# The first queries' load and transposes, moved from GpSimd and float16 to SyncE and float32

## The chip, the cores and the metric

The kernel runs on one core of a Trainium2 chip. A core has five engines with instruction streams of their own: TensorE (PE, matmuls; its weight loads are shown apart as PEld), VectorE (DVE), ScalarE (ACT), GpSimd (POOL) and SyncE (SP, which only issues DMAs here). Sixteen DMA engines move data between the chip's memory (HBM) and the core's SBUF. The metric is the device time of one execution in microseconds, less being better; a value given for a kernel is the median of its runs.

## The reference

Two stages follow each other. The first is an attention over blocks: a Sinkhorn normalization turns `sort_net` into soft permutations, which mix the blocks of keys and values; then each block of queries attends to one mixed block. The second is a mixture of four two-layer networks, weighted by normalized probabilities.

```python
def _attn_ref(q, k, v, sort_net):          # q, k, v: (4, 8, 768, 64); sort_net: (4, 8, 8, 8)
    P = sort_net
    for _ in range(5):
        P = np.exp(P - np.max(P, axis=-1, keepdims=True))
        P = P / (np.sum(P, axis=-1, keepdims=True) + 1e-09)
        P = P / (np.sum(P, axis=-2, keepdims=True) + 1e-09)
    k_sorted = np.einsum('bhij,bhjcd->bhicd', P, k_b)   # k_b, v_b: blocks of 96 rows
    v_sorted = np.einsum('bhij,bhjcd->bhicd', P, v_b)
    scores = scale * np.matmul(q_b, k_sb.transpose(0, 1, 2, 4, 3))
    attn = softmax(scores)                               # over the 96 keys of the block
    return np.matmul(attn, v_sb)

def _moe_ref(x, domain_probs, w1, w2):     # x: (3072, 512); w1: (4, 512, 1024); w2: (4, 1024, 512)
    p = domain_probs / (domain_probs.sum(-1, keepdims=True) + 1e-09)
    out = np.zeros((N, D))
    for e in range(4):
        out += p[:, e:e + 1] * (np.maximum(x @ w1[e], 0.0) @ w2[e])
    return out
```

All inputs and the output are float32 in HBM. `x` is the attention's output with the heads of a token side by side.

## The kernel before

The instructions of each engine run in the order in which the kernel's text issues them; semaphores are put in where one engine needs what another or a DMA has made. No scheduler moves anything. There are two sets of PSUM buffers, `psM` and `psA`, of two buffers each, handed out in turn.

**Loads.** GpSimd issues nearly all loads, since those cast float32 to float16 on the way (`load_natural` for k and v, `load_half_queries` for batch 0's queries, `load_w1` and `load_w2` for the networks' weights). Its DMAs use eight semaphores in turn, so from the ninth on an issue also waits until the DMA eight places before it has landed. SyncE issues loads without a cast, stores and DMA transposes. At the start SyncE issues `sort_net` into `sn` (L77), then the probabilities twice, in two layouts: `p_in` (L170) and `p_own` (L171). GpSimd issues, in this order: the first halves of the queries of quads 0 and 1 (L172, through L152; a quad is four heads), the first k quad (L173), then it makes the identity matrix `ident` in float16 (L177), and issues the first v quad, the second k quad, the second v quad (L178 to L180), and four pieces of the first network's `w1` (L183).

The queries of batch 0 lie in `q0`, a view of the scratch tile `Tt[3]`: partitions 0 to 63 hold quad 0, 64 to 127 quad 1, and on each of them are two halves of the sequence, four heads, six blocks' rows and 64 columns of float16.

**Start.** PE has nothing to do until the Sinkhorn iterations are through. `warm(n)` (L272) issues `n` matmuls of a constant tile, 128x128 by 128 columns, whose result nobody reads. The text issues `warm(84)` (L307), then the five iterations (L309 to L327): an exponential on ScalarE (L310), then on VectorE row sums, reciprocal, product, column sums, reciprocal (L315 to L319) and, but for the last iteration, another product (L321). After iterations 1 to 3, VectorE also takes one step each of `spread_weights` (L244): the sum over `p_in` (L246), an addition (L248) and a reciprocal (L250). In the last iteration, between the exponential and the row sums, the text issues `h_q(0, 0, nc.scalar.copy)` and `h_q(1, 0, nc.scalar.copy)` (L313) and `warm(30)`.

`h_q` (L280) transposes the half queries of a quad: 24 transposes of 64x64 on PE (L288), through `ident`, into one PSUM tile, and one copy of it by ScalarE into `qT0[qd]` (L292).

**What follows.** After the iterations VectorE and GpSimd write half of the normalized matrix each, spread over 16 columns (L330); PE transposes it (`r_half`, L342), VectorE builds block-diagonal matrices from it (`build_PI0`, L353), and PE mixes k and v with these, quad by quad (`mix_half`, L521). Scores (`h_s`, L576), exponentials (L582), the transposes of v (`h_w`, L548), the products with v (`h_a`, L593) and the transposes of the result (`h_x`, L624) follow, and from about 18 us on the first layer of network 0 (`group0`, L704) is put between them. `h_s` reads `qT0`. The second halves of the queries are loaded at L1405, into the other half of `q0`, and transposed near 29 us by `h_q_both`. The tile `room` takes outputs of network 0 later on (L747).

All else (the other batches' attention and the networks, whose products are built from fewer block products with sums of blocks) fills the rest of the span with matmuls.

Of the kernel before, what the change touches and what calls it, by code (L numbers as in the profile page):

```python
# [10 lines left out]
F32 = mybir.dt.float32  # L11
# [7 lines left out]
def kernel(  # L19
# [11 lines left out]
    nc = tc.nc  # L31

    B, H, S, D = q.shape
# [6 lines left out]
    P = 128  # L40
# [3 lines left out]
    R = BLK // CP  # L44
# [23 lines left out]
    def psa(shape, dtype, name):  # L68
        state["n"] += 1
        return psA.tile(shape, dtype, tag="ps", name=name)  # L70
# [16 lines left out]
    def from_spare(n):  # L87
        at = spare["at"]
        spare["at"] += n
        return Sflat[:, ds(at, n)]  # L90
# [5 lines left out]
    q0 = Tt[3].rearrange("p a f x -> p (a f x)").rearrange("p (f h r d) -> p f h r d", f=2, h=4, r=R)  # L96
# [4 lines left out]
    room = const.tile([P, 4, Dm], F32, name="room")  # L101
    arena = const.tile([P, 4 * NW + NQ + 4 * 4 * P + R * 4 * VW], F16, name="arena")

    def half_queries(qd, hf):
        return q[0, ds(4 * qd, 4)].rearrange("h (p r) d -> p h (r d)", r=R)[ds(64 * hf, 64)]

    def load_natural(b, nm, qd, parts=1, between=None):
        src = {"k": k, "v": v}[nm]
        t = arena[:, ds(("k", "v").index(nm) * 2 * NW + qd * NW, NW)].rearrange("p (h r d) -> p h r d", h=4, r=R)
        natural[(b, nm, qd)] = t  # L110
        n = 4 // parts
        for m in range(0, 4, n):
            nc.gpsimd.dma_start(
                t[:, ds(m, n)].rearrange("p h r d -> p h (r d)"),
                src[b, ds(4 * qd + m, n)].rearrange("h (p r) d -> p h (r d)", r=R),
            )
            if m == 0 and between:
                between()
# [31 lines left out]
    def load_half_queries(hf):  # L150
        for qd in range(2):
            nc.gpsimd.dma_start(  # L152
                q0[ds(64 * qd, 64), hf].rearrange("p h r d -> p h (r d)"), half_queries(qd, hf)
            )
# [7 lines left out]
    def p_part(at, n):  # L162
        return Tt[2].rearrange("p a f x -> p (a f x)")[:, ds(2 * at, 2 * n)].bitcast(F32)
# [3 lines left out]
    p_den = p_part(2 * E * NT, NT).rearrange("p (t o) -> p t o", o=1)  # L167
    p_own = p_part(2 * E * NT + NT, R * E).rearrange("p (t e) -> p t e", e=E)
    own_den = p_part(2 * E * NT + NT + R * E, R).rearrange("p (t o) -> p t o", o=1)
    nc.sync.dma_start(p_in, moe_domain_probs.rearrange("(p t) e -> p t e", t=NT))  # L170
    nc.sync.dma_start(p_own, moe_domain_probs[0:S].rearrange("(t p) e -> p t e", p=P))  # L171
    load_half_queries(0)  # L172
    load_natural(0, "k", 0)  # L173


    ident = const.tile([P, P], F16, name="ident")
    make_identity(nc, ident)  # L177
    load_natural(0, "v", 0)  # L178
    load_natural(0, "k", 1)
    load_natural(0, "v", 1)  # L180
# [63 lines left out]
    def spread_weights():  # L244

        nc.vector.tensor_reduce(p_den, p_in, AX.X, ALU.add)  # L246
        yield
        nc.vector.tensor_scalar(out=p_den, in0=p_den, scalar1=1e-9, scalar2=None, op0=ALU.add)  # L248
        yield
        nc.vector.reciprocal(p_den, p_den)  # L250
        yield
        nc.vector.tensor_tensor(
            p_out.rearrange("p e t -> p t e"), p_in, p_den.broadcast_to([P, NT, E]), ALU.mult
        )
        p_rows = p_dram.rearrange("e (p t) -> p e t", t=NT)
        nc.sync.dma_start(p_rows[0:S_P], p_out[0:S_P])
        pbs[(0, 0)] = load_p(0, 0)
        nc.sync.dma_start(p_rows[S_P:P], p_out[S_P:P])
        yield
# [12 lines left out]
    def warm(n):  # L272
        ps = psM.tile([P, 4, P], F32, tag="ps", name=f"ps_w_{state['n']}")
        state["n"] += 1
        for m in range(n):
            nc.tensor.matmul(ps[:, m % 4, :], dummy, dummy, start=True, stop=True)

    qT0 = [from_spare(2 * S).rearrange("p (s f r x) -> p s f r x", s=2, f=2, r=R) for _ in range(2)]

    def h_q(qd, hf, copy, ps=None):  # L280

        if ps is None:
            ps = psa([P, 2, R, 64], F16, f"ps_q_{qd}_{hf}")
        rows = ds(64 * qd, 64)
        for sg in range(2):
            for r in range(R):
                for hh in range(2):
                    nc.tensor.transpose(  # L288
                        ps[ds(D * hh, D), sg, r, :], q0[rows, hf, 2 * sg + hh, r, :], ident[rows, rows]
                    )  # L290
        if copy:
            copy(qT0[qd][:, :, hf], ps[:])  # L292

    def h_q_both(hf, copy):

        ps = psa([P, 2, 1024], F16, f"ps_q_{hf}")
        pss = [ps[:, qd, 0:2 * R * 64].rearrange("p (s r x) -> p s r x", s=2, r=R) for qd in range(2)]
        for qd in range(2):
            h_q(qd, hf, None, pss[qd])
        for qd in range(2):  # L300
            copy[qd](qT0[qd][:, :, hf], pss[qd])
# [2 lines left out]
    srow = const.tile([GH, NB, 1], F32, name="srow")  # L304
    scol = const.tile([GH, NB, 1], F32, name="scol")
    sn16 = const.tile([GH, NB, NB, CP], F16, name="sn16")
    warm(84)  # L307
    p_steps = spread_weights()
    for it in range(5):  # L309
        nc.scalar.activation(sn[:], sn[:], AF.Exp, bias=0.0, scale=1.0)  # L310
        if it == 4:
            for qd in range(2):
                h_q(qd, 0, nc.scalar.copy)  # L313
            warm(30)
        nc.vector.tensor_reduce(srow[:], sn[:], AX.X, ALU.add)  # L315
        nc.vector.reciprocal(srow[:], srow[:])
        nc.vector.tensor_tensor(sn[:], sn[:], srow[:].broadcast_to([GH, NB, NB]), ALU.mult)
        nc.vector.tensor_reduce(scol[:], sn[:].rearrange("p i j -> p j i"), AX.X, ALU.add)
        nc.vector.reciprocal(scol[:], scol[:])  # L319
        if it < 4:  # L320
            nc.vector.tensor_tensor(  # L321
                sn[:], sn[:],
                scol[:].rearrange("p j o -> p o j").broadcast_to([GH, NB, NB]),
                ALU.mult,
            )
            if it:
                next(p_steps)  # L327
# [1146 lines left out]
    def load_w2_part(e, d):  # L1474
# [6 lines left out]

    later = [
        [(h_q_both, 1, (vec, act)), (h_w, 1, vec)],
        [(h_s, 0, 2), (h_s, 1, 2)],
        [(h_w, 0, vec)],
# [92 lines left out]
```

## Time and profile before

| | |
|---|---|
| median of 3 runs | 358.08 us (358.04 to 359.21) |
| profiled execution | 358.21 us |
| its span | 356.3 us |
| PE busy | 350.4 us |
| VectorE, ScalarE, GpSimd busy | 277.5, 170.1, 137.6 us |

The profile is that of one execution. Its span runs from the first to the last instruction of the program; 1.9 us of the execution's time lie around it. A row of a timeline reads: start in us, duration in us, engine, line of the kernel, operation, written tile <- read tiles, shapes, count, and in brackets the engine's idle time before it and what ended it. The view of waits sums such idle times. "Landing" is the time from a DMA's issue to its arrival.

### The profile page before, as it was taken

Reading aid. Unit: us, or ns where it says so; the run is one execution under the profiler, and the core shown is the slowest. Engines: PE = TensorE matmul, PEld = TensorE weight load, DVE = VectorE, ACT = ScalarE, POOL = GpSimd, SP = SyncE. Lnnn points to the kernel's source line nnn. Section 1 sums busy time; section 2 is a strip of 40 time slices with the busy share of each in tenths; the row PEclk is TensorE's granted clock in tenths of the full one; section 3 lists DMA queues with packets and bytes.
Section 4 is the critical chain, followed back from the end, with each engine's and each line's share of the span. In section 5 each row is a group of like instructions: output and inputs, shape, how many; then the busy total and the mean of one; then the engine's idle time right before and its main releaser. Section 6 shows DMA issues by size and latency. Waiting matters only on the chain.

```text
span 356.3 us, 9511 instructions
## 1 busy us (share of the span) xinstructions
PE 350.4 (98%) x3948; PEld 305.5 (86%) x3948; DVE 277.5 (78%) x555; ACT 170.1 (48%) x302; POOL 137.6 (39%) x154
## 2 busy tenths in 40 slices
PE   8899999999999999999999999999999999999996
PEld 8686857888888888988899888888888888888886
DVE  5766787779798687778879988896678886588963
ACT  2653330452425445368847259830288611598301
POOL 8766112466022420000626318840068800188400
PEclk9999999999999999999999999999999999999999
DMA  8999999999999999743995410005200014100021
GB/s 104 203 205 230 212 209 194 207 195 167 195 180 166 195 116 203 138 88 44 180 205 91 107 74 0 2 1 136 78 26 3 2 37 141 62 0 2 0 75 46
DMA packets 74762, 40.26 MB, mean 113 GB/s; under 512 B 41568, under 2 KB 70496, under 8 KB 74720
## 3 DMA queue, kind: packets, MB, share of 16 engines
q0 software_dynamic: 38720, 19.93, 43.2%
q1 hardware_dynamic: 35856, 19.67, 27.2%
q8 instruction: 31, 0.51, 0.6%
q14 instruction: 11, 0.09, 0.1%
q10 hardware_dynamic: 144, 0.07, 0.1%
HBM read 41.88 MB, written 6.34 MB: 135 GB/s over the span
## 4 chain that ended last, share of the span: by engine, by line
PE 95%; DVE 3%; issue 0%; DMA 0%; ACT 0%; DVEq 0%
PE ps_h L815 18%; PE ps_Q L1296 18%; PE ps_p L799 12%; PE ps_X L1153 10%; PE ps_Z L1153 7%; PE ps_Q L1153 7%; PE ps_Z L1296 6%; PE ps_h L704 3%; PE ps_o L741 3%; PE ps_p L860 3%; PE ps_a L479 2%; PE ps_s L444 2%; PE ps_k L425 1%; PE ps_v L391 1%; PE ps_mv L521 1%; PE ps_a L593 0%
## 5 line engine op out<-in xcount | busy, mean ns | idle before, releaser
L815 PE MATMUL ps_h<-xT,w 128*128 128x256 f16 x576 | 67.5, 273 | 0.0
L815 PEld LDWEIGHTS <-w 128*128 128x128 f16 x576 | 55.2, 98 | 7.3
L821 DVE SCALAR_TENSOR_TENSOR Hb<-ps_h,pb 128x1024 f16<-128x1024 f32 x34 | 41.5, 1223 | 17.8 <-PE ps_h L815 17.6
L1153 PEld LDWEIGHTS <-w 128*128 128x128 f16 x480 | 43.6, 98 | 4.7
L1166 POOL TENSOR_TENSOR arena<-tmp,pb 128x512 f16<-128x512 f32 x12 | 15.2, 1276 | 65.7 <-PE ps_Z L1153 49.8
L1296 PEld LDWEIGHTS <-Hb 128*128 128x128 f16 x320 | 31.1, 98 | 3.5
L1165 ACT ACTIVATE tmp<-tmp 128x512 f32<-128x512 f32 x46 | 29.0, 632 | 3.9 <-DVE tmp L1203 3.9
L1296 PEld LDWEIGHTS <-Sb 128*128 128x128 f16 x304 | 28.2, 98 | 3.0
L1153 PEld LDWEIGHTS <-arena 128*128 128x128 f16 x312 | 27.7, 98 | 2.8
L451 ACT ACTIVATE ET<-ps_s 96x768 f16<-96x768 f32 x24 | 18.1, 802 | 25.2 <-PE ps_s L444 25.0
L434 ACT CAST kT<-ps_k 64x384 f16<-64x384 f32 x48 | 22.7, 473 | 13.3 <-PE ps_k L425 12.3
L126 POOL DMA_DIRECT2D arena<-in_q_dram x24 | 19.9, 842 | 20.8 <-DMA q_ring<-arena 17.7
L1153 PE MATMUL ps_X<-ET,arena 128*128 128x256 f16 x168 | 25.2, 272 | 0.0
L1296 PE MATMUL ps_Q<-w,Hb 128*128 128x256 f16 x192 | 24.6, 273 | 0.0
L799 PEld LDWEIGHTS <-Hb 128*128 128x128 f16 x232 | 21.9, 98 | 3.0
L1159 DVE SCALAR_TENSOR_TENSOR Hb<-ps_X,pb 128x512 f16<-128x512 f32 x27 | 18.7, 692 | 7.0 <-PE ps_X L1153 7.0
L1173 ACT COPY ps_X<-ps_Z 128x512 f32<-128x512 f32 x27 | 15.4, 571 | 17.8 <-PE ps_Z L1153 17.8
L1153 PE MATMUL ps_Z<-xT,w 128*128 128x256 f16 (+1 forms) x176 | 22.5, 258 | 0.0
L785 DVE TENSOR_TENSOR Sb<-Hb 128x512 f16<-128x512 f16 x33 | 20.6, 646 | 0.0
L1180 ACT COPY tmp<-ps_X 128x512 f32<-128x512 f32 x26 | 15.2, 586 | 9.2 <-PE ps_X L1153 6.6
L1159 DVE SCALAR_TENSOR_TENSOR Hb<-ps_Z,pb 128x512 f16<-128x512 f32 x27 | 18.4, 683 | 1.3 <-PE ps_Z L1153 1.3
L1203 DVE TENSOR_TENSOR tmp<-ps_Q,tmp 128x512 f32<-128x512 f32 x26 | 17.7, 683 | 0.8 <-PE ps_Q L1153 0.8
(270 smaller groups left out, 744.3 us busy)
## 6 DMA issues: line engine op xcount, KB each, us to landing
w<-in_moe_w_dram POOLq DMA_DIRECT2D x4, 1024.0 KB, 27.2
w<-in_moe_w_dram POOLq DMA_DIRECT2D x6, 512.0 KB, 19.7
arena<-in_k_dram POOLq DMA_DIRECT2D x7, 384.0 KB, 7.6
arena<-in_v_dram POOLq DMA_DIRECT2D x7, 384.0 KB, 8.1
vs<-arena SPq DMA_DIRECT2D x36, 66.0 KB, 5.3
arena<-in_q_dram POOLq DMA_DIRECT2D x24, 96.0 KB, 7.5
out_dram<-ob SPq DMA_DIRECT2D x9, 256.0 KB, 2.0
pb<-p_dram SPq DMA_DIRECT2D x4, 512.0 KB, 5.8
```

The costliest lines, as they stand in the source:

```text
L126: nc.gpsimd.dma_start(t[:, h // 2, :, h % 2, :], q[b, h].rearrange("(t p) d -> p t d", p=P))
L434: nc.scalar.copy(kT[ds(D * hh, D), r], pk[ds(D * r, D), hh].rearrange("p a (i c) -> p a i c", c=CP),)
L451: nc.scalar.activation(ETs[2 * (pr % 2) + hh][:, 0:S].rearrange("c (a x) -> c a x", a=2), pss[hh][0:BLK, :, 0:HS], AF.Exp, bias=0.0, scale ...
L785: tt(sm[0], blk(0, 1), blk(1, 1), ALU.add)
L799: nc.tensor.matmul(ps, lhs(e, f), Ts[e][rhs][:, f, :], start=(first and e == es[0] and f == 0), stop=(done and e == es[-1] and f == KH - 1 ...
L815: nc.tensor.matmul(ps[:, f, :], w1sb[e][:, kc, ds((4 * g + f) * P, P)], xT[:, kc, ds(2 * c * P, 2 * P)], start=(kc == 0), stop=(kc == NKC ...
L821: nc.vector.scalar_tensor_tensor(out=Hb[:, homes.get(e, e), ds(4 * g, 4), :], in0=ps[:], scalar=0.0, op0=ALU.max, in1=weights(e).broadcast ...
L1153: nc.tensor.matmul(dst[:, ds(f * cols, cols)], a[lhs][:, k, ds((f0 + f) * P, P)], t[rhs][:, k, :], start=(first and f == 0 and k == 0), st ...
L1159: nc.vector.scalar_tensor_tensor(out=home(i, j), in0=src.rearrange("p (f x) -> p f x", f=m), scalar=0.0, op0=ALU.max, in1=weight(j).broadc ...
L1165: nc.scalar.activation(src, src, AF.Relu, bias=0.0, scale=1.0)
L1203: tt(t12, Q, u2, ALU.add)
L1296: nc.tensor.matmul(ps, lhs(e, f), Ts[e][rhs][:, f, part], start=(first and e == 0 and f == 0), stop=(e == E - 1 and f == KH - 1), skip_gro ...
```

## The change

The first half of quad 0's queries is no longer loaded by GpSimd with a cast. SyncE loads it as float32, as its second DMA, into `q32`: partitions 0 to 63 of `q0`, both halves of the sequence's room, read as float32. GpSimd's DMA for quad 1 stays. GpSimd also copies a 64x64 corner of `ident` into a corner of `room` as float32, `ident32`. A new function `h_q32` transposes quad 0's half queries by 24 float32 matmuls (the queries as stationary operand, `ident32` as the moving one) into a float32 PSUM tile. It is issued ahead of the iterations, behind `warm(60)` in the place of `warm(84)`. In the last iteration ScalarE copies its result into `qT0[0]`, quad 1's transposes follow as before, and `warm(28)` stands for `warm(30)`. The second half of quad 0's queries is still loaded at the same place, over `q32`.

```diff
+    q32 = q0[0:64].rearrange("p f h r d -> p (f h r d)").bitcast(F32).rearrange("p (h r d) -> p h r d", h=4, r=R)
+    nc.sync.dma_start(q32.rearrange("p h r d -> p h (r d)"), half_queries(0, 0))
     nc.sync.dma_start(p_in, moe_domain_probs.rearrange("(p t) e -> p t e", t=NT))
     nc.sync.dma_start(p_own, moe_domain_probs[0:S].rearrange("(t p) e -> p t e", p=P))
-    load_half_queries(0)
+    nc.gpsimd.dma_start(q0[ds(64, 64), 0].rearrange("p h r d -> p h (r d)"), half_queries(1, 0))
     load_natural(0, "k", 0)
     ident = const.tile([P, P], F16, name="ident")
     make_identity(nc, ident)
+    ident32 = room[0:64, 0, 0:64]
+    nc.gpsimd.tensor_copy(ident32, ident[0:64, 0:64])
     load_natural(0, "v", 0)
...
+    def h_q32():
+
+        ps = psa([P, 2, 512], F32, "ps_q32")
+        for sg in range(2):
+            for r in range(R):
+                for hh in range(2):
+                    nc.tensor.matmul(
+                        ps[ds(D * hh, D), sg, ds(r * 64, 64)], q32[:, 2 * sg + hh, r, :], ident32, start=True, stop=True
+                    )
+        return ps[:, :, 0:R * 64].rearrange("p s (r x) -> p s r x", r=R)
...
-    warm(84)
+    warm(60)
+    ps_q32 = h_q32()
     p_steps = spread_weights()
     for it in range(5):
         nc.scalar.activation(sn[:], sn[:], AF.Exp, bias=0.0, scale=1.0)
         if it == 4:
-            for qd in range(2):
-                h_q(qd, 0, nc.scalar.copy)
-            warm(30)
+            nc.scalar.copy(qT0[0][:, :, 0], ps_q32)
+            h_q(1, 0, nc.scalar.copy)
+            warm(28)
```

## The prediction

> **What bounds the kernel now.** I read the page first: engines, granted clock, chain.
>
> ```profile
> span 356.3 us, 9511 instructions
> PE 350.4 (98%) x3948; PEld 305.5 (86%) x3948; DVE 277.5 (78%) x555; ACT 170.1 (48%) x302; POOL 137.6 (39%) x154
> PEclk9999999999999999999999999999999999999999
> ```
>
> TensorE (PE) is busy 98% of the span at the full granted clock. The table of windows then tells where the other 2% lies; its columns are the stretch, its length, and each engine's busy time in it.
>
> ```profile
> 0.00:10.00 10.00, 8.94 (x159) 8.80 (x160) 6.18 (x30) 2.96 (x7) 8.70 (x19) 1.00 0.87 113
> 10.00:20.00 10.00, 8.17 (x204) 6.88 (x202) 6.95 (x19) 6.08 (x11) 7.67 (x19) 1.00 1.28 204
> 20.00:40.00 20.00, 19.89 (x351) 14.87 (x348) 12.92 (x25) 9.30 (x13) 10.92 (x14) 1.00 1.23 219
> 40.00:60.00 20.00, 20.00 (x162) 14.18 (x161) 17.47 (x29) 4.84 (x6) 3.02 (x5) 1.00 1.32 203
> ```
>
> From 40 us on PE has no idle time that this view shows. What the change touches lies before 17 us, so it can move the end only by moving the point from which PE runs without a break. The chain of waits shows what sets that point (columns: start, duration, what).
>
> ```profile
> 10.64 0.20 DVE scol L319
> 10.86 0.69 DVE sn L330
> 11.55 0.05 issue
> 11.60 0.26 PE ps_R L342 x4
> ```
>
> Up to 11.55 the chain is the Sinkhorn iterations on VectorE and ScalarE. No query and no TensorE work is in it. What PE does beside them is in PE's timeline:
>
> ```profile
> 1.06 6.74 PE L276 MATMUL ps_w<-Hb 128*128 128x128 f16 x84 [1.06 <-DVE Hb L157]
> 7.73 0.85 PE L288 MATMUL ps_q<-ident,T 64*64 64x64 f16 x48
> 8.51 1.85 PE L276 MATMUL ps_w<-Hb 128*128 128x128 f16 x30
> 11.60 0.26 PE L342 MATMUL ps_R<-ident,sn 32*128 32x32 f16 x4 [1.24 <-DVE sn L330]
> 14.40 0.57 PE L521 MATMUL ps_mk<-Sb,arena 128*64 128x64 f16 x24
> 16.15 0.57 PE L521 MATMUL ps_mv<-Sb,arena 128*64 128x64 f16 x24
> ```
>
> The 48 transposes of the first queries start right behind the 84 dummies: they waited for no load. PE then idles 1.24 us for the Sinkhorn result. The last two lines are the first uses of the second k and v quads. Their loads, by the DMA view cut to the issue of each (columns: KB, us from issue to landing):
>
> ```profile
> arena<-in_k_dram POOLq DMA_DIRECT2D x1, 384.0 KB, 9.3
> arena<-in_v_dram POOLq DMA_DIRECT2D x1, 384.0 KB, 10.5
> T<-in_q_dram POOLq DMA_DIRECT2D x1, 192.0 KB, 4.3
> ```
>
> k was issued at 4.88 and landed at 14.2, v at 5.62 and 16.1, the second quad's queries at about 1.93 and 6.2. All landed before their use, but v by only 0.05 us.
>
> **The change part by part.**
>
> *Dummies and float16 transposes that go (PE).* The 30 dummies took 1.85 us with the last one's latency of about 0.2 inside, so 0.056 each. 24 of the first batch's last dummies are 1.34 us; the 60th ends at 7.73 - 1.34 = 6.39. Half of the 48 transposes is about 0.4 (0.85 / 48 = 17.7 ns each), two later dummies 0.11. Removed: 1.85 us, all in PE's shadow of the Sinkhorn chain.
>
> *Float32 transposes that come (PE).* No row shows a float32 matmul. In the compiled program each of the 24 is two weight loads and two matmuls, 48 of each. Bounds: the float16 pairs give 48 x 17.7 ns = 0.85 us. If nothing overlapped, each pair would cost its weight load and its matmul in full; the line of L288 gives these:
>
> ```profile
> L288 PEld LDWEIGHTS <-T x48: 103/110/110, 7.7 to 8.4; 64*64 64x64 f16 x48
> L288 PE MATMUL ps_q<-ident,T x48: 192/193/213, 7.7 to 8.4; 64*64 64x64 f16 x48
> ```
>
> That is 48 x 0.30 = 14.4 us, an end which no PE row comes near, since each of them overlaps loads with matmuls. I take twice to four times the float16 price, as elements are twice as wide and the two halves of one tile can't run side by side as two neighbouring tiles do: 1.7 to 3.4 us, middle 2.5.
>
> *The room for it.* From 6.39 to 11.60 are 5.21 us; less 0.4 for the remaining float16 transposes, 0.1 for a change of shape, and 28 x 0.056 = 1.56 for the later dummies, 3.15 us are left, 131 ns for each float32 transpose. At 2.5 us PE ends at about 10.95 and still waits 0.65 us for the Sinkhorn result: cost 0. At 3.4 us it is 0.25 late. The cover is the Sinkhorn chain; whatever PE exceeds 3.15 us by moves everything behind it.
>
> The row says 0.85 us when 48 float16 pairs are the measure. [...]
>
> *Queries' load on SyncE's queue.* 384 KB instead of 192, since nothing is cast. Issued at 1.21, behind the 8 KB of sort_net and ahead of both probability loads; it takes an issue of 0.40 us there, so p_in goes out at about 1.66 and p_own at 2.1. Landing: the output stores of the same queue land 256 KB in 2.0 us, so 3.0 us for 384 KB at the quick end (4.2); the gpsimd query load's 4.3 us is the slow end (5.5). The DMA share is 0.22 to 0.35 between 2 and 3.5 us, so I take the quick end. The transposes begin at 6.39: cost 0 at either.
>
> *p_in behind it.* VectorE's reduction of p_in stands in the Sinkhorn chain's engine order, at 5.72; everything of the chain is queued behind it. p_in's packets ran 2.5 to 3.0 us; behind the queries it lands at 4.7, or 6.0 at the slow end. Cost 0, bound 0.3. p_own is first used at 21.1.
>
> *GpSimd's queue.* One DMA issue less (0.66), one 64x64 copy more (about 0.3, by the 0.29 of the 128x128 copy, L194): 0.4 us earlier for all behind it. The identity in float32 is there by about 4. GpSimd's half of L330 began at 11.23, 0.4 after its input; it would end at 12.1 instead of 12.46, but PE comes to it at 13.33 behind two blocks of matmuls. Gain 0. The k and v loads come up to 1.0 us earlier (192 KB at about 192 KB per us), and with them the weight loads, whose issues wait for them. Since PE waited for none, gain 0, bound -1.0. The copy of room's corner is read long before room is next written, past 31 us.
>
> *ScalarE.* The first evacuation reads float32: by the 0.81 of the 768-wide L582 against 0.73, +0.08. It ends near 11.1; ScalarE's next work is at 13.05 after 2.08 us idle. Cost 0, unless PE is over 2 us late.
>
> *Sum.* 358.21 us for the profiled execution (span 356.3 and 1.9 around it) + 0. The median of the runs shown is 358.08, so 358.1 is forecast. 0.5%, 1.8 us, is about what a measurement of this kernel can tell from no change.
>
> **The rivals.**
>
> *PE is late (slower).* The float32 weight loads do not hide behind matmuls. Price: 48 x 0.103 = 4.94 on the 1.70 us, 6.6 in all, 3.5 us over the room: 361.6. It decides from 131 ns for each transpose, and passes 0.5% at (3.15 + 1.8) / 24 = 206 ns. For it: alternating tiles hid the float16 loads, while here the second load of a tile comes while its first half still runs. Against it: L521 hides its loads at 15 to 16 ns for each matmul at the same 64 columns.
>
> *p_in is late (slower).* SyncE's queries run into gpsimd's stream, and the chain stands at 5.72. Worked above: up to 0.3, and 0.9 if its 8 packets on each DMA engine also take turns with gpsimd's 0.08 us ones: 358.4 to 359.0.
>
> *The clock falls (slower).* If the float32 phase is short, PE is idle from 9.3 to 11.6, 2.3 us instead of 1.24. If the granted clock fell to half there, as it visibly was for the first dummies (38 in the first 3.94 us, about 0.105 each against 0.056), some 1.7 to 3.4 us of matmuls between 11.6 and 15.6 would be added: 359.8 to 361.5. The row shows no fall over 1.24 us. [...]
>
> *The loads did matter (faster).* If the 0.05 us of slack of v hides a wait, the ramp gains up to the 1.0 us of the stream: 357.1. Against it: the gap before 16.15 is the ordinary 0.09 us of a change of shape.
>
> **How the numbers follow.** PE in time, 358.1: 64%. PE late: 22%, 5 of them under 1.8 us and 17 beyond, as no row fixes the price. p_in late: 5%, 1 beyond. Clock: 4%, beyond. Loads: 5%, 2 of them beyond 0.5% by more than I can work out. So faster 2%, same 64 + 5 + 4 + 3 = 76%, slower 22%. The range goes from 357.0, the loads' gain, to 360.6, where float32 transposes take 0.235 us each (5.65 us, 2.5 over the room); left out are some 10 of PE late, 2 of the clock and 2 below.
>
> **What would show it.** In the changed kernel's PE timeline: float32 transposes starting at about 6.4 straight behind the dummies, lasting 1.7 to 3.4 us, and a line L342 (moved in number) at 11.6 still released by VectorE. VectorE's reduction of p_in at 5.7 without idle time. k and v landing up to 1.0 us earlier with no PE start moved. Wrong it would be if L342 starts late behind PE's own work, if the Sinkhorn steps shift, or if PE's dummies after 11.6 take 0.1 us each.

## The result and the profile after

The changed kernel takes 360.74 us (median of 6 runs, 360.14 to 361.38) against 358.15 us (6 runs, 358.04 to 359.21). The ratio is 1.0067, with a 95% interval of 1.0050 to 1.0085: slower, by 2.6 us. The forecast was no change, 358.1 us, in a range from 357.0 to 360.6. The median lies 0.1 us above that range; the ratio times the 358.08 us from which the forecast was counted gives 360.5, just inside it. So the kernel is slower where no change was forecast, by more than the 0.5% which the prediction called the same.

The profiled execution took 360.42 us with a span of 358.2 us, 1.9 us more than before. PE's busy time did not grow:

```profile
span 358.2 us, 9510 instructions
PE 350.5 (98%) x3946; PEld 305.7 (85%) x3946; DVE 277.5 (77%) x555; ACT 170.1 (47%) x302; POOL 137.5 (38%) x154
PEclk9899999999999999999999999999999999999999
```

Two things stand there already: the same matmul time in a longer span, so PE waits more, and one slice of the granted clock (the second, 9 to 18 us) below full speed. The chain of waits has a DMA in it now (columns: start, duration, what):

```profile
1.21 0.74 SPq L171
...
2.00 4.90 DMA T<-in_moe_domain_probs_dram
...
6.92 0.25 DVE T L250
...
11.99 0.69 DVE sn L346
...
12.73 0.26 PE ps_R L358 x4
```

SyncE's issue of the queries comes first, then p_in's DMA, then VectorE's sum over it, then the rest of the Sinkhorn iterations. Lines have moved: L250 was L246, L346 was L330, L358 was L342. The wait is in VectorE's timeline, with its idle time and its cause in brackets:

```profile
5.85 0.21 DVE L337 TENSOR_TENSOR sn<-sn,scol 32x64 f32<-32x64 f32 x1
6.92 0.25 DVE L250 TENSOR_REDUCE T<-T 128x24 f32<-128x96 f32 x1 [0.86 <-DMA T<-in_moe_domain_probs_dram]
7.09 0.20 DVE L331 TENSOR_REDUCE srow<-sn 32x8 f32<-32x64 f32 x1
```

Before, the same reduction started at 5.72 with no idle time. The next iteration's row sum stood behind it: its exponential ended at 6.36, and it started at 7.09; before, it started at 6.11, 0.03 us behind its exponential. PE's timeline shows what follows:

```profile
1.06 5.16 PE L280 MATMUL ps_w<-Hb 128*128 128x128 f16 x60 [1.06 <-DVE Hb L157]
6.87 1.44 PE L304 MATMUL ps_q<-room,T 64*64 64x64 f32 x42 [0.64 <-DMA T<-in_q_dram]
8.59 1.74 PE L280 MATMUL ps_w<-Hb 128*128 128x128 f16 x28
12.73 0.26 PE L358 MATMUL ps_R<-ident,sn 32*128 32x32 f16 x4 [2.40 <-DVE sn L346]
```

PE ends its dummies at 10.3 as before, but the Sinkhorn result comes at 12.73 instead of 11.60, and PE idles 2.40 us instead of 1.24. Then the clock falls. The table of windows (stretch, its length, busy time of PE, weight loads, VectorE, ScalarE, GpSimd, then granted clock, DMA share, GB/s):

```profile
11.37:14.78 3.41, 2.01 (x68) 1.78 (x70) 2.17 (x7) 1.23 (x4) 2.74 (x3) 1.00 1.30 202
14.78:18.19 3.41, 3.41 (x64) 2.78 (x66) 2.12 (x5) 2.41 (x5) 3.29 (x5) 0.50 1.24 206
18.19:21.60 3.41, 3.17 (x72) 2.75 (x68) 2.14 (x6) 2.38 (x4) 2.37 (x6) 1.00 1.28 201
```

For exactly 3.41 us PE has half its clock. Laid against each other matmul by matmul, the two traces give the sum of the loss: the first transpose of the Sinkhorn result (ps_R) is 1.13 us late, the second v quad's matmuls, near the end of the half-clock stretch, 1.87 us, and from there to 31 us it stays at 1.92. So 1.1 us come from the late chain and 0.8 us from the clock.

Not all of the 1.1 us is the wait for p_in. Before it, the chain was 0.28 us late already, nearly all of it because `sort_net` landed later. That differs between executions: the first exponential started at 2.30 us in this profile of the kernel before, and at 2.48 us in that of the experiment on idle time alone, which has the same loads. The wait added 0.70 us, and one VectorE product that took 0.37 instead of 0.21 us the rest.

The loss has a third part, at the other end of the kernel. Of the 1.92 us, PE gains 0.37 back at 31 and 65 us (why is open): the last matmul starts at 354.76 us instead of 353.22. But from there to the end of the span 3.48 us pass instead of 3.04. SyncE's records in the trace end with ten instructions that wait for semaphores, one behind the other. Before, the one for the last store is the ninth of them; now it is the second, and the eight others follow it at about 0.06 us each. All seven profiled kernels that have the additional load on SyncE show 3.47 or 3.48 us; the kernel before and the one of the experiment on idle time alone, which do not have it, 3.04 and 3.08. So about 0.4 us go with the additional DMA, wherever it stands in the queue; that it shifts the semaphores that SyncE's DMAs get is read from these records and was not tested.

In three of the six runs the mean clock is 0.990 instead of 0.995, the same as in the profile of the run with 8 dummies below, which has two such stretches, and their span is 1.0 us longer still.

### The profile page after: what moved, and what is told of

Same layout as the page of the kernel before. It is cut to its first block, busy times and chain, and to the rows that moved or that the text cites. A ratio compares the mean times of both kernels' runs of the same rounds, so it can differ in the third digit from the quotient of the medians.

```text
span 358.2 us, 9510 instructions
## 1 busy us (share of the span) xinstructions
PE 350.5 (98%) x3946; PEld 305.7 (85%) x3946; DVE 277.5 (77%) x555; ACT 170.1 (47%) x302; POOL 137.5 (38%) x154
## 4 chain that ended last, share of the span: by engine, by line
PE 95%; DVE 2%; DMA 1%; SPq 0%; issue 0%; ACT 0%; DVEq 0%
PE ps_h L831 18%; PE ps_Q L1312 18%; PE ps_p L815 12%; PE ps_X L1169 10%; PE ps_Z L1169 7%; PE ps_Q L1169 7%; PE ps_Z L1312 6%; PE ps_o L757 3%; PE ps_h L720 3%; PE ps_p L876 3%; PE ps_a L495 2%; PE ps_s L460 2%; DMA T<-in_moe_domain_probs_dram 1%; PE ps_k L441 1%; PE ps_v L407 1%; PE ps_mk L537 1%
## 5 line engine op out<-in xcount | busy, mean ns | idle before, releaser
L1189 ACT COPY ps_X<-ps_Z 128x512 f32<-128x512 f32 x27 | 15.4, 571 | 17.8 <-PE ps_Z L1169 17.8
L1219 DVE TENSOR_TENSOR tmp<-ps_Q,tmp 128x512 f32<-128x512 f32 x26 | 17.7, 682 | 0.8 <-PE ps_Q L1169 0.8
```

The lines of the kernel that those rows point to most:

```text
L1219: tt(t12, Q, u2, ALU.add)
```

## The experiments

The theory after this reading: p_in, queued behind the queries on SyncE, lands too late; VectorE waits for it in the middle of the Sinkhorn chain; PE's longer idle time then costs the clock. The rival: the float32 transposes, or the larger load's share of the DMA engines, cost the time by themselves.

**p_in ahead of the queries.**

```diff
-    nc.sync.dma_start(q32.rearrange("p h r d -> p h (r d)"), half_queries(0, 0))
     nc.sync.dma_start(p_in, moe_domain_probs.rearrange("(p t) e -> p t e", t=NT))
+    nc.sync.dma_start(q32.rearrange("p h r d -> p h (r d)"), half_queries(0, 0))
```

> The changed kernel with one swap on SyncE's queue: p_in is issued second, the float32 queries third. Theory A (p_in's lateness starts the loss): p_in lands by about 3.5 us, VectorE's reduction of p_in has no idle time before it, the first transposed matrix part (r_half) starts at 11.6 to 11.9 instead of 12.73; PE's idle time before it is about 1.2 us plus what PE waits for the queries, which land at 7 or a little later; the clock stays granted; 358.1 to 358.6 us. Theory B (the float32 transposes or their load cost the time by themselves, through the clock or through the shared DMA engines): the clock still falls near 15 us and the time stays above 359.3 us.

Measured: 358.92 us against 358.34, ratio 1.0012 (1.0004 to 1.0021). VectorE's and PE's timelines:

```profile
5.84 0.23 DVE L250 TENSOR_REDUCE T<-T 128x24 f32<-128x96 f32 x1
```
```profile
7.65 1.44 PE L304 MATMUL ps_q<-room,T 64*64 64x64 f32 x42 [1.24 <-DMA T<-in_q_dram]
11.84 0.26 PE L358 MATMUL ps_R<-ident,sn 32*128 32x32 f16 x4 [0.73 <-DVE sn L346]
```

No wait before the reduction, full clock throughout, although the same load and the same float32 transposes are there and PE even waits 1.24 us for the queries. The mean clock of all eleven runs is 0.998 to 1.000. The swap takes away most of the loss, 0.55 of 0.67%, and with it the rival's loss at the start. The median is 0.3 us above the first theory's range, and 0.12% (0.4 us) stay. That fits the third part above: this profile has 3.47 us behind the start of its last matmul. Its ps_R is 0.24 us late, half of that from sort_net's landing; with the loads unchanged, in the experiment on idle time alone, it is 0.21 us late as well.

**The late p_in, but nobody waiting for it.**

```diff
-            if it:
+            if it > 1:
                 next(p_steps)
...
     next(p_steps)
+    next(p_steps)
     group0(0, 1, 0, [0, 1])
```

> The changed kernel with the steps of the probabilities taken after iterations 2 and 3 only (the third one later, beside the fourth), so that VectorE first needs p_in at about 7.6 instead of 5.7 us. SyncE's queue, all loads, the float32 transposes and the dummies stay as they are. Theory A (what is lost is VectorE's wait in the Sinkhorn chain, not the lateness itself): p_in lands at 6.9 again, no idle time before its reduction, r_half at 11.6 to 11.9, clock granted, 358.1 to 358.9 us. Theory B (the larger load slows the start through the DMA engines, or the float32 transposes cost time): the time stays above 359.5 us.

Measured: 358.67 us against 358.40, ratio 1.0004 (0.9996 to 1.0013): no difference from the kernel before. p_in was issued at 2.01 and took 5.2 us, so it landed at 7.2, no earlier than in the changed kernel, but VectorE came to it at 7.77. PE's row of ps_R follows:

```profile
7.77 0.23 DVE L250 TENSOR_REDUCE T<-T 128x24 f32<-128x96 f32 x1
```
```profile
11.88 0.26 PE L358 MATMUL ps_R<-ident,sn 32*128 32x32 f16 x4 [1.11 <-DVE sn L346]
```

SyncE's queue, the loads, the float32 transposes and the dummies are those of the changed kernel. The mean clock of all twelve runs is 0.999 or 1.000. So what it loses at the start hangs on where one 0.23 us reduction stands in VectorE's order; the third part, 0.44 us at the end, is in this profile too, and the interval leaves room for it.

**The extra load alone, in the kernel before.**

```diff
+    nc.sync.dma_start(
+        room[0:64].rearrange("p a d -> p (a d)")[:, 0:4 * R * D].rearrange("p (h x) -> p h x", h=4), half_queries(0, 0)
+    )
     nc.sync.dma_start(p_in, moe_domain_probs.rearrange("(p t) e -> p t e", t=NT))
```

> The kernel before with one load added, which nobody reads: the same 384 KB of queries as float32 on SyncE's queue between sort_net and p_in, into the unused room tile. No float32 matmul, no change in GpSimd's queue, 84 and 30 dummies. Theory A: p_in lands at 6.9 us or later (GpSimd's stream still has both query loads), the Sinkhorn chain is 1.1 us or more late, PE idles 2.4 us, the clock may fall: 359.2 without and 360.0 to 361.4 us with the fall. Theory B (the float32 transposes matter): 358.1 to 358.5 us.

Measured: 361.84 us (360.47 to 365.0), ratio 1.0105 (1.0074 to 1.0135).

```profile
7.72 0.25 DVE L249 TENSOR_REDUCE T<-T 128x24 f32<-128x96 f32 x1 [1.74 <-DMA T<-in_moe_domain_probs_dram]
```
```profile
13.56 0.26 PE L345 MATMUL ps_R<-ident,sn 32*128 32x32 f16 x4 [3.16 <-DVE sn L333]
```

With both of GpSimd's query loads still in place, p_in is later than in the changed kernel, VectorE waits 1.74 us, ps_R is 1.96 us late, and the clock is halved for 6.83 us, two stretches. Without a single float32 matmul the loss is there, and larger: the first theory, beyond its upper time of 361.4.

**Idle time alone, in the kernel before.**

```diff
-            warm(30)
+            warm(8)
```

> The kernel before with 8 dummies instead of 30 behind the transposes: PE idles about 2.5 us before r_half, which stays at 11.6. Theory A (idle time costs the clock): the granted clock falls to 0.5 for a stretch of some 3.4 us between 12 and 19 us, and the time rises by 0.5 to 1.7 us, to 358.7 to 359.9. Theory B (idle time of 2.5 us does not matter; it takes float32 matmuls): no fall, 358.1 to 358.3 us.

Measured: 359.89 us (358.67 to 360.62), ratio 1.0039 (1.0024 to 1.0054). Nothing was changed but dummies which nobody reads, and the clock shows it: the mean is 0.986 to 0.995 in all six runs, against 0.999 or 1.000 in the 17 of the kernel before beside them. In the profile PE waits for ps_R, then two stretches have half the clock, where one was expected:

```profile
11.81 0.26 PE L342 MATMUL ps_R<-ident,sn 32*128 32x32 f16 x4 [1.71 <-DVE sn L330]
```
```profile
13.80:17.20 3.40, 3.39 (x61) 2.74 (x63) 2.16 (x5) 2.37 (x5) 2.36 (x4) 0.51 1.26 205
17.20:20.60 3.40, 3.40 (x61) 3.10 (x60) 1.32 (x4) 2.51 (x4) 1.92 (x4) 0.50 1.26 203
```

ps_R is 0.21 us late there, and the first layer's matmuls, at 20.50 instead of 18.61 us, 1.89 us. The idle time was only 1.71 us and not the 2.5 expected, because the first 84 dummies ran 1 us longer, 7.71 us instead of 6.74 (their end is at 8.7 instead of 7.7).

**More dummies in the changed kernel.**

```diff
-            warm(28)
+            warm(62)
```

> The changed kernel with 62 dummies instead of 28 behind the transposes, so that PE is busy until about 12.2 us. Theory A (p_in's lateness makes PE idle for 2.4 us, and the idle time costs the clock): p_in is as late as before, r_half starts at 12.73 still, but the clock stays granted through 15 to 18 us and the 0.8 us lost there come back: 359.3 to 359.7 us. Theory B (float32 matmuls, not idle time, cost the clock): the fall near 15 us stays, 360.1 to 361.4 us.

Measured: 361.9 us (361.72 to 363.18 in four of five executions; the fifth took 368.68), ratio 1.0112 (1.0094 to 1.0129). It agrees with neither theory: the clock held in the profile (the idle time before ps_R is 0.54 us), but the time got worse. PE's waits of this kernel show two that were nowhere before (columns: us in total, times, longest):

```profile
PE ps_mv L564 <- issue: 0.9, 1, 0.9
PE ps_R L358 <- DVE sn L346: 0.5, 1, 0.5
PE ps_q L292 <- issue: 0.4, 1, 0.4
```

"issue" is time in which the profile shows nothing that PE waits for. The two stops, at 18.5 and 31.4 us, lie behind the 351st and the 607th matmul, 256 matmuls with their weight loads apart, and the traces have loads of 16 KB on the instruction queue at about these times: 17.2, 23.2 and 29.2 us in the kernel before, 17.4, 23.9 and 30.6 us in the changed one. Over the two stops PE falls from 1.13 to 2.83 us behind the kernel before. What PE lacks there is not shown; this run has 34 more pairs, and the next one tests whether it is their number.

**Wider dummies instead of more.**

```diff
+        four = dummy.rearrange("p (o x) -> p o x", o=1).broadcast_to([P, 4, P])
+        for m in range(wide):
+            nc.tensor.matmul(ps[:], dummy, four, start=True, stop=True)
...
-            warm(28)
+            warm(14, wide=14)
```

> The changed kernel with 14 of the 28 later dummies made four times as wide (128x512 columns), so that PE is busy until about 12.4 us with the same number of instructions as the changed kernel (the run with 62 dummies had 34 matmuls and weight loads more). Theory A (the clock's share comes from idle time, and the extra loss of the run with 62 dummies from PE's longer instruction stream): r_half at 12.73 as in the changed kernel, clock granted through 15 to 18 us, no idle time on PE marked issue; 1.1 us over the kernel before at r_half and about as much at the end: 359.2 to 359.7 us. Theory B (the run with 62 dummies lost by being warm where memory or another engine could not follow): the same stalls of 0.4 to 1.1 us between 18 and 32 us, 361 us or more.

Measured: 359.73 us (359.64 to 360.00) against 358.40, ratio 1.0034 (1.0022 to 1.0047): at the upper end of the first theory's range.

```profile
8.86 3.19 PE L281 MATMUL ps_w<-Hb 128*128 128x512 f16 x14
11.89 0.94 PE L283 MATMUL ps_w<-Hb 128*128 128x128 f16 x14
12.85 0.26 PE L361 MATMUL ps_R<-ident,sn 32*128 32x32 f16 x4
```

PE has no idle time before ps_R, the clock is full from then on, and no wait marked issue is left: the stops of 0.9 and 0.4 us came with the number of instructions. ps_R is 1.25 us late, the kernel's end 1.3. This separates the clock from the rest of the loss: 0.34% with the wait and the longer end, 0.67% with the clock besides.

**The queries' load with the DMA engines to itself.** GpSimd's first loads were issued behind its mask and memset work (from 3.55 us on instead of 1.27).

```diff
-    nc.gpsimd.dma_start(q0[ds(64, 64), 0].rearrange("p h r d -> p h (r d)"), half_queries(1, 0))
-    load_natural(0, "k", 0)
...
+    nc.gpsimd.dma_start(q0[ds(64, 64), 0].rearrange("p h r d -> p h (r d)"), half_queries(1, 0))
+    load_natural(0, "k", 0)
+    load_natural(0, "v", 0)
...
     vo = arena[:, ds(4 * NW + NQ + 4 * 4 * P, R * 4 * VW)].rearrange("p (r h w) -> p r h w", r=R, h=4)
```

> The changed kernel with all of GpSimd's first loads issued behind its mask and memset work, some 3 us later, so that SyncE's query load has the DMA engines to itself for longer. Only the landing of the queries and of p_in is of interest; the time will be longer by 2 to 4 us, as k and v come late. Theory A (queries and p_in are late because every packet of SyncE's queue takes turns with one of GpSimd's): from the first packets at 2.75 us the 256 packets of 1536 bytes need 1.0 to 1.4 us, the queries land by about 4.5 instead of 6.7 us and p_in by 4.8 instead of 6.9. Theory B (the queue starts slowly by itself: the packets before 4 us take 0.2 us each whoever else is there): few packets up to 4 us as in the changed kernel, then full speed, queries by about 5.5 and p_in by about 5.8 us.

One execution took 359.5 us, beside 358.39 for the kernel before, so 1.1 us more and not the 2 to 4 expected: the second k and v quads, issued only 1.4 us later than in the changed kernel, landed at 14.0 and 16.0 us. VectorE waited 0.30 us for p_in, ps_R was 0.14 us late, and the clock fell behind an idle time of 1.74 us. The DMA view, cut to SyncE's issues of this kernel (KB, us from issue to landing):

```profile
T<-in_q_dram SPq DMA_DIRECT2D x1, 384.0 KB, 4.7
T<-in_moe_domain_probs_dram SPq DMA_DIRECT2D x1, 48.0 KB, 4.1
```

The queries land at 5.9 instead of 6.7 us and p_in at 6.1 instead of 6.9. So having the DMA engines to itself brings the landing 0.8 us forward, and it still comes later than either theory said. The single packets show where the rest lies. Before 3.5 us each takes about 0.12 us here (0.2 us in the changed kernel), from then to 4.2 us 0.065. The last packet of the queries ends at 4.72 us and p_in's at 4.99 (6.07 and 6.23 in the changed kernel), near the first theory's times; but the landings, which are the arrival of the last semaphore update, come 1.2 and 1.1 us behind these packets (0.7 us in the changed kernel, 0.3 for p_in in the kernel before). What holds the updates up is open.

## Where the prediction was wrong, and what held

**The step that failed is the landing of the queries, and p_in's behind them.** The prediction took 4.2 us for the queries from the output stores' 2.0 us for 256 KB, with 5.5 as the slow end, and from these 4.7 or 6.0 for p_in, "cost 0, bound 0.3". Both ends were too early:

```profile
T<-in_q_dram SPq DMA_DIRECT2D x1, 384.0 KB, 5.5
T<-in_moe_domain_probs_dram SPq DMA_DIRECT2D x1, 48.0 KB, 4.9
```

Issued at 1.21 and 2.00, they landed at 6.7 and 6.9. The row used for the quick end is the median of nine stores between 146 and 353 us, in the other direction, and the DMA share in the 2 us from their issues was 0.33 to 0.61 but for one at 1.37, against 1.14 to 1.36 from 4 to 7 us in the changed kernel; the slow end was a load of half the bytes. The issues themselves took 0.74 and 0.59 us, not 0.40. (In the kernel before, p_in's packets ran from 2.24 to 2.67 us; the 3.0 us of the prediction is their landing.) The place was named rightly: VectorE's reduction at 5.72, with the whole chain behind it. The rival "p_in is late", at up to 0.9 us, had the size (0.86 us of VectorE's wait, 0.70 of it passed on to the chain), and was given 5%.

**The clock was a rival of its own, and should have been the second half of that one.** The prediction tied it to a short float32 phase and gave it 4%. It came with the idle time that the late chain made, 2.40 us, and stayed away where dummies filled that time (0.54 us with 62 of them, none with the wide ones). Its price was put at 1.7 to 3.4 us, the author's estimate, which no run shows; one stretch cost 0.8 us in the profile. The 3.41 us of half clock hold what took 2.6 us before, so that part of that time was not stretched; waits between engines would explain it, which is an argument and no measurement. Two rivals that share a cause make one case whose prices add.

The forecast of no change would have been in doubt even with the queries in time. With the transposes at their measured 1.44 us and a start at 6.39, the prediction's own sum lets PE end at 9.9 us and idle for 1.7 until 11.6. Two profiles have that idle time, 1.71 and 1.74 us, the second of them with ps_R only 0.14 us late, and in both the clock fell. A run with the queries that early was not made.

**The float32 transposes** were sized at 1.7 to 3.4 us. The row above has 42 of their 48 matmuls in 1.44 us; the other six start between float16 ones, and the last ends at 8.48, 1.61 us behind the first start. From start to start a pair of weight load and matmul takes 29.7 ns, a float16 pair 14.0, so that a transpose of two pairs costs 4.2 times a float16 one. (The prediction's 17.7 ns has the last matmul's latency in it.) In the trace before, the float16 matmuls of two neighbouring tiles mostly start 3 or 4 ns apart, and the next two 28 or 29 ns later; the float32 ones, behind their first two, start 36 and 23 ns apart by turns. The 1.70 us in the price of "PE is late" is twice the float16 row, an estimate that no run shows; the runs showed the 1.61 us above. So "PE is late", which held 17 of the 22 points for slower, did not happen: PE ended its dummies at 10.3. Slower came about by another way than the one that it was forecast by, and that the time lies at the edge of a range whose upper end stands for slow transposes is luck.

**What held.** The loads bring nothing: the second k quad was issued at 4.47 and landed at 13.5 instead of 14.2, the second v quad at 15.4 instead of 16.1, and in the two kernels without VectorE's wait, whose loads come as early, the matmuls between 11.8 and 19.5 us keep a constant distance of 0.2 to 0.3 us behind those of the kernel before. PE's waits show no load of k or v in any of these kernels. ScalarE's first evacuation took 0.77 us instead of 0.73; GpSimd's loads of w1 began at 5.94 instead of 6.35, the 0.4 us forecast. Both are hidden. The 0.4 us behind the last matmul stood in no term of the sum, nor in a rival.

## What to carry to other kernels

A load put ahead of others on a queue must be costed for what stands behind it: here 384 KB made 48 KB late, and one reduction of 0.25 us, with the Sinkhorn steps behind it on VectorE, carried that into the critical chain. Take the landing of a first load from loads at the kernel's start, not from stores at its end, and move the consumer if the load has to be late: that alone brought the time back to within the interval of 0.13%. A late chain can cost more than its lateness: here it was 1.13 us late, PE idled for 2.40 us, its granted clock then fell to 0.50 for 3.41 us, and that cost 0.8 us more. And look at both ends of the trace: an additional DMA at the start also moved the waits at the end.

## What the runs showed of the hardware

- The granted clock was halved for 3.41 us in the changed kernel, and for 6.83 us in the run with 8 dummies and in that with the extra load. In the profiled executions idle times before ps_R of 1.71 us (8 dummies), 1.74 (queries alone), 2.40 (changed kernel) and 3.16 (extra load) went with a fall, those of 0.54 us (62 dummies), 0.73 (p_in first), 1.11 (later reduction) and 1.24 (kernel before) did not. In the changed kernel the fall came at 14.78 us, 2.05 us after the start of ps_R; in the run with 8 dummies ps_R started at 11.81, and the stretch from 13.80 to 17.20 has a mean of 0.51. (One of the 34 runs of the kernel before beside the experiments, 359.66 us, shows a mean clock of 0.995 too.) What else decides on a fall is not shown.
- With 34 more pairs of weight load and matmul PE stopped for 0.9 and 0.4 us later on, 256 pairs apart; with 14 of 28 dummies made four times as wide instead, and no more pairs, it did not. The cause of the stops is not shown.
- SyncE's issue of the queries took 0.74 us, against 0.40 us for sort_net and for p_in before; p_in's, behind it, took 0.59 us.
- From the end of a load's last packet to its landing 0.3 us passed for p_in in the kernel before, 0.7 us in the changed kernel, and 1.1 us with GpSimd's loads held back.
- Of SyncE's waits for semaphores at the end of the program, eight follow that for the last store in the changed kernel, at about 0.06 us each, and one in the kernel before; from the last matmul's start to the end of the span 3.48 us pass instead of 3.04.
